# Smaller first units, row sums inverted on VectorE, normalisation in halves, and a new order of work in a planned attention and MLP kernel

## The chip, the core and the metric

The kernel runs on one core of a Trainium2 chip. Its engines have queues of their own: TensorE (PE in the profile; its weight loads are PEld), ScalarE (ACT), VectorE (DVE), GpSimd (POOL), and SyncE (SP), which only issues DMAs here. The metric is device time in microseconds, the median of several runs. A change of less than about 0.2%, or 1.5 us, can't be told from none.

## The reference

The input x has 2048 rows of 640 numbers. One branch is attention with 32 heads of 20 columns, the other an MLP with 1536 hidden columns and the activation mish. A sigmoid of x times a weight vector mixes them, row by row. All inputs are bf16.

```python
g = _sigmoid((x * gate_w).sum(-1, keepdims=True))
qkv = (x @ wqkv)...                                  # 32 heads of 20
scores = jnp.einsum("bhqd,bhkd->bhqk", q, k) * scale
p = _softmax(scores, axis=-1)
a = jnp.einsum("bhqk,bhkd->bhqd", p, v) ... @ wo
h = jnp.einsum("bsd,df->bsf", x, w1) + b1
b = jnp.einsum("bsf,fd->bsd", h * jnp.tanh(softplus(h)), w2)
return g * a + (1 - g) * b
```

The exponential of 32 x 2048 x 2048 scores is the bulk of the elementwise work.

## The kernel before

**Units and slots.** Heads are taken in 8 groups of 4 (`HG`), queries in 4 columns of 512 (`CW`). A group of a column, `(c, g)`, has 16 tiles of 128 keys. A *unit* `(c, g, kt, j)` is the score tile of head `j` for one tile of keys and the 512 queries: one matmul into one PSUM bank (`score_mms`, L1378). `subs` tells which matmuls a unit has. The last group is cut in two halves of 256 queries, and there a unit is 256 keys by 256 queries, made by two matmuls. Three units are a *slot*. There are 683 slots, and their scores take turns in banks 0 to 2 and 3 to 5.

**Who takes the exponential.** ACT takes a slot with one instruction (L1400), over three banks (1536 columns) or over two (1024). In the second case the slot's third unit was given to DVE by `choose`: DVE writes it as a 16-bit integer that is read as an fp16 number (`emit_x`, L1450). A batch of four such units gets two more passes over 2048 columns (`close`, L1488), since the value used is the sum of three such approximations. PE then multiplies by V (`pv`, L1720) into one bank for each group. A column of ones in V makes the row sums beside the products.

**Normalising a group** (`group_done`). DVE copies the bank to `OUNG` (L1905). A DMA collects the sums into `RR` (128x16). `invert` takes one over them: a power of -1 on GpSimd (L1927). A DMA writes `RR` to DRAM (`SUMS`), and four more spread it over the partitions into `BCT` (`spread`, L1936). One product `OUNG` x `BCT` follows, on DVE or on GpSimd (`times`, L1857). There is one `OUNG`. 31 groups go this way; the two cut halves at the end are transposed and inverted on DVE instead.

**The MLP's mish** is one tanh on ACT for each of 24 pieces (L1071), and then scalar steps (L1095) and four products (L1104) on 1024 fp16 columns. A product may be split in four: quarters to GpSimd, the rest to DVE.

**Who sets the order.** All of this is written out ahead of time. A planner (`Plan`) has a model of each engine's clock and adds instructions one by one. The numbers at the top of the file are its costs, due times and thresholds. `choose(s)` refuses to give a unit to DVE when DVE's modelled clock is too far ahead of ACT's: the variable `late` is DVE's lead less an allowance in `NUDGE`, one entry for each 8 slots. `settle` gives a job to GpSimd when it fits, by the modelled clocks, between two DVE instructions of kind "L" (those that work on SBUF alone) and would be done before DVE's modelled clock. `patient(op, wait)` holds DVE off from the same job until its clock is `wait` past the job's input: `AWAIT` (0) for the product with `BCT`, `AWAIT_2` (0.2) for a product of mish. `fill_up` puts matmuls into PE's idle time: while the streaming time that it modelled in the last `WINDOW` (4.8 us) is under `SPUN` (0.95) of it, and the filler bank is idle, it adds a matmul that nothing uses (`spin`, L2152).

**The start** (`first_keys`, `second_keys`). Two DMAs bring 256 rows of x each, PE turns them (L837), and DVE and ACT copy them to `XB` (L814 and L815). Then PE makes Q of group 0 for the low 256 rows and for the high 256, and K for the low 256 (L850). DVE copies K in two pieces of 128. The scores of slots 0 and 1 follow, then K of the high rows (`second_keys`, L818), then V of the first 512 rows (L887), and only then slot 2.

Of the kernel before, what the change touches and what calls it, by code (L numbers as in the profile page):

```python
# [17 lines left out]
P = 128  # L18
# [8 lines left out]
NFT = D // P  # L27
NFC = NF // P
NC = 4
CW = 512  # L30
NHC = 8
HW = 256
# [16 lines left out]
HOP = 0.1  # L49
# [5 lines left out]
STREAM = 0.38  # L55
SPUN = 0.95
# [6 lines left out]
PARTS = 1  # L63
MPARTS = 4
AWAIT_2 = 0.2
TAKE_M = 1
APART = 0.1
LANDED = 1.6
SEEN = 10
SPREAD_TAIL = 2.1  # L70
SUMS_TAIL = 1.1
FLEX = 1
TOP_UP = 0
SX = 305
SX_STEP = 1
AWAIT = 0
SHARE = 0.3
AWAIT_1 = 0
CALM_END = 90
# [12 lines left out]
GIVE_BACK = 50  # L92
# [6 lines left out]
STORED = 2  # L99
TALL = 0.1  # L100
BEYOND = 0.4
SOONER = 8
# [5 lines left out]
AHEAD = 20  # L108
# [6 lines left out]
CATCH_UP = 18  # L115
BUSY = 0.8
CROWD = 1.2
MARGIN = 2.5
EAGER = 85
LOAD = 0.95  # L120
MISH = 3.75
GROUP = 2.25
LAST = 0
END = 45
SHIFT = 0.6
LAG = 15
SPARE = 11
WINDOW = 4.8
# [11 lines left out]
OVER = 0  # L140
DIRECT = 1
FEW = 4
PART_DUE = 48
LAST_DUE = 29
# [21 lines left out]
NUDGE = [-5.3, -2.3, -2.8, 0.7, 4.4, 3.7, -3.0, 0.7, -3, 2.2, 2.2, -0.7, -0.7, 2.3, 0.8, -1.5, 4.5, 0.0, 6, 0, -0.7, -6, 0, 0, 2.1, 1.4, 0.7, 3.7, 0.7, 1.4, 5.2, 0.0, 4.4, 0, 4.7, 3, 3.7, 1.4, 6, 6, 6, 6, 2.3, 4.5, -0.8, -0.1, -0.8, 2.3, 0, 2.3, 1.4, 0, 2.2, 0, 0, 2.2, 1.5, 5, 2.9, 5.1, -0.8, 2.2, -3, 4.5, -5.7, -1.5, -0.1, -1, 4.5, 6, 6, 1.4, -4.3, 2.1, 4.9, 0.7, 0.7, 0.7, 0.0, -1.4, 5, 3.5, 6, 4.3, -1.5, -1.5, 1.5]  # L166
# [116 lines left out]
def bass_gated_mix__softmax_full_mha__dense_activation_mish__prompt_kernel(  # L283
# [154 lines left out]
    def attention(pl, fast):  # L438
# [97 lines left out]
        def safe(op):  # L536

            return op.t1 + HOP + RISK[op.eng]
# [78 lines left out]
        if fast:  # L617
# [206 lines left out]
            first_more = []  # L824

            def first_keys():
# [4 lines left out]
                def turn(half, pair):  # L831
# [9 lines left out]
                    by = ("dve", "act", "act") if half is lows else ("dve", "act", "dve")  # L841
# [6 lines left out]
                def mms(bank, pads, half, deps):  # L848
                    for f in range(NFT):
                        last = pl.add("pe", lambda e, f=f: e.matmul(  # L850
                            PS[:, bank, 0:HW], pads[:, 0, f, :], xt(0)[:, f, half], start=(f == 0), stop=(f == NFT - 1)),
                            [moved[(half is highs, f)], *deps], cost=HW * COL)
                    return last
# [17 lines left out]
                return pl.add("dve", lambda e: e.memset(PS[:, ACC, :], 1.0), [moved[(True, 4)]], cost=0.5)  # L871
# [157 lines left out]
            u_free = [None]  # L1029
# [36 lines left out]
            def mish(ev, hb, hc, k):  # L1066
# [9 lines left out]
                def piece(cost, fn, after=None, wait=0):  # L1076
                    def run(eng="dve", *more):
                        last[0] = pl.add(eng, fn, [last[0], *more], cost=ASIDE_1 if more else cost, kind="L")
# [9 lines left out]
                def done(op):  # L1088
                    h_done[(hc, k - 1)] = h_done[(hc, k)] = op
# [242 lines left out]
        def emit_s(s):  # L1332
            deps = [e_op.get(s - 2), ev_op.get(s - 2)]
            deps += [bank_free.get(SLOT * (s % 2) + i) for i in range(SLOT)] if s < 2 else []
            for c, g, kt, j in slots[s]:
                if fast:
                    deps += [k_done[(real(g), subs(c, g, kt)[-1][0] // 4)], q_done[(real(g), c)]]
                if fast and (c, g) == (0, 0) and 2 <= kt < 4:
                    deps += k_more
                if fast and s == 1:  # L1340
                    deps += first_more
# [24 lines left out]
        def score_mms(s, some, deps):  # L1366

            op = None
            for r in range(max(len(subs(*u[:3])) for u in some)):
                began = set()  # L1370
                for i, (c, g, kt, j) in enumerate(some):
# [3 lines left out]
                    cost = max(extent(c, g)[1] * COL, THIN)  # L1375
# [171 lines left out]
        def choose(s):  # L1547

            late = max(0.0, pl.now["dve"] - pl.now["act"]) - NUDGE[s // 8]
# [154 lines left out]
        def pv(some):  # L1704
# [3 lines left out]
            w = extent(c, g)[1]  # L1708
            bank = sums_at[(c, g)]
            for r in range(CW // w):  # L1710
                for n, ((_, _, kt, j), src, deps, scaled_v) in enumerate(some):
                    tile, cols, of_q = subs(c, g, kt)[r]
                    if not any(started.get((c, g, i)) for i in range(HG)):
                        deps = [*deps, bank_free.get(sums_at[(c, g)])]
                    if fast:
# [7 lines left out]
                        cost=0.004 if n else max(w * COL, THIN), kind="V")  # L1723
# [93 lines left out]
        def group_done(c, g, step, last):  # L1817
# [108 lines left out]
            def invert():  # L1926
                r = (pl.add("pool", lambda e: e.tensor_tensor(  # L1927
                    RR[:, :], RR[:, :], NEG[:, :].to_broadcast([P, 16]), ALU.pow), [got, m_neg], cost=INVERT)
                     if fast else pl.add("dve", lambda e: e.reciprocal(RR[:, :], RR[:, :]), [got], cost=0.25))
# [33 lines left out]
        if fast:  # L1963
# [3 lines left out]
            for s in range(2):  # L1967
                compose(s)
                emit_s(s)
# [455 lines left out]
```

## Time and profile before

| | |
|---|---|
| Median of 3 runs | 753.92 us (753.31 to 754.74) |
| Profiled execution: device time / span | 755.81 us / 754.0 us |
| ACT busy | 736.5 us, 98% |
| PE / DVE / POOL busy | 94% / 93% / 25% |
| Granted TensorE clock, mean | 0.998 |
| Exponentials on ACT: of 3 units / of 2 | 191 / 492 |
| Power of -1 on POOL | 31 times, 93.9 us |

In the groups of instructions, the name of a row is the line, the engine, the operation, and what is written from what. After the count stand the busy time, the mean nanoseconds of one, and the engine's idle time just before. Instructions of one engine overlap at their ends, so the step from start to start is shorter than the duration. In the chain of waits, a row is a piece of the work that ended last, with start and length. In a table by stretches, the numbers beside an engine are its busy time and its count.

### The profile page before, as it was taken

Reading aid. Unit: us, or ns where it says so; the run is one execution under the profiler, and the core shown is the slowest. Engines: PE = TensorE matmul, PEld = TensorE weight load, DVE = VectorE, ACT = ScalarE, POOL = GpSimd, SP = SyncE. Lnnn points to the kernel's source line nnn. Section 1 sums busy time; section 2 is a strip of 40 time slices with the busy share of each in tenths; the row PEclk is TensorE's granted clock in tenths of the full one; section 3 lists DMA queues with packets and bytes.
Section 4 is the critical chain, followed back from the end, with each engine's and each line's share of the span. In section 5 each row is a group of like instructions: output and inputs, shape, how many; then the busy total and the mean of one; then the engine's idle time right before and its main releaser. Section 6 shows DMA issues by size and latency. Waiting matters only on the chain.

```text
span 754.0 us, 19649 instructions
## 1 busy us (share of the span) xinstructions
PE 707.4 (94%) x8065; PEld 266.4 (35%) x8065; DVE 703.4 (93%) x1298; ACT 736.5 (98%) x715; POOL 188.6 (25%) x162
## 2 busy tenths in 40 slices
PE   8999999999998999999999999999999999999996
PEld 4334333333332343233333334333333333323232
DVE  4878898999898999989999999999999999999995
ACT  6999999999999999999999999999999999999996
POOL 8111101333212420212213322213204232223111
PEclk9999999999999999999999999999999999999999
DMA  8321321321233215112113302102222122011001
GB/s 188 105 63 42 99 70 35 101 67 53 65 107 101 70 47 163 39 42 56 54 44 108 95 21 73 60 21 76 82 55 71 55 60 80 20 33 31 18 18 47
DMA packets 81675, 49.62 MB, mean 66 GB/s; under 512 B 25474, under 2 KB 77562, under 8 KB 81578
## 3 DMA queue, kind: packets, MB, share of 16 engines
q1 hardware_dynamic: 80810, 48.16, 22.7%
q8 instruction: 67, 1.10, 0.6%
q14 instruction: 30, 0.25, 0.1%
q10 hardware_dynamic: 656, 0.10, 0.1%
q0 software_dynamic: 112, 0.01, 0.0%
HBM read 36.10 MB, written 7.52 MB: 58 GB/s over the span
## 4 chain that ended last, share of the span: by engine, by line
ACT 86%; PE 7%; DVE 3%; DMA 2%; POOL 0%; issue 0%; SPq 0%
ACT ETS L1400 83%; ACT REG L1071 2%; PE PS L1378 2%; PE PS L1720 2%; PE PS L575 2%; ACT W2R L1071 1%; DVE QT L1450 1%; DMA OTN<-in_A_x_dram 1%; DMA SUMS<-RR 1%; DMA BCT<-SUMS 1%; DVE KT L1450 0%; PE PS L785 0%; POOL RR L1927 0%; DMA RR<-OUNG 0%; PE PS L2152 0%
## 5 line engine op out<-in xcount | busy, mean ns | idle before, releaser
L1400 ACT ACTIVATE ETS<-PS 128x1024 bf16<-128x1024 f32 (+1 forms) x683 | 715.7, 1263 | 5.4 <-PE PS L1378 4.9
L1378 PE MATMUL PS<-QT,KT 32*128 32x512 bf16 (+1 forms) x2112 | 267.3, 378 | 34.0 <-ACT ETS L1400 23.7
L1927 POOL TENSOR_TENSOR RR<-RR,NEG 128x16 f32<-128x16 f32 x31 | 93.9, 3029 | 268.8 <-DMA RR<-OUNG 268.8
L1720 PE MATMUL PS<-ETS,V_all 128*21 128x512 bf16 (+1 forms) x1606 | 156.8, 375 | 0.0
L1378 PEld LDWEIGHTS PS<-QT,KT 32*128 32x128 bf16 x2112 | 67.7, 91 | 250.4 <-ACT ETS L1400 212.1
L1104 POOL TENSOR_TENSOR U<-U 128x256 f16<-128x256 f16 x77 | 50.9, 661 | 215.6 <-DVE U L1095 176.8
L1450 DVE TENSOR_SCALAR QT<-PS 128x512 int16<-128x512 f32 x123 | 82.4, 682 | 2.6 <-PE PS L1378 1.9
L575 PE MATMUL PS<-XB,REG 128*32 128x256 bf16 (+3 forms) x824 | 80.5, 294 | 2.0 <-DVE OUTT L1185 1.5
L1450 DVE TENSOR_SCALAR OTN<-PS 128x512 int16<-128x512 f32 x109 | 73.3, 681 | 2.3 <-PE PS L1378 2.0
L575 PE MATMUL PS<-W2R,HB 128*128 128x320 bf16 (+1 forms) x645 | 72.4, 300 | 0.2
L1450 DVE TENSOR_SCALAR PADS<-PS 128x512 int16<-128x512 f32 x101 | 67.9, 682 | 4.8 <-PE PS L1378 4.6
L575 PEld LDWEIGHTS PS<-XB,REG 128*32 128x32 bf16 (+1 forms) x824 | 39.5, 97 | 32.1 <-issue 21.1
L1720 PEld LDWEIGHTS PS<-ETS,V_all 128*21 128x21 bf16 x1606 | 39.1, 90 | 30.0 <-issue 25.5
L575 PEld LDWEIGHTS PS<-W2R,HB 128*128 128x128 bf16 (+1 forms) x645 | 33.1, 97 | 29.1 <-issue 14.7
L1450 DVE TENSOR_SCALAR KT<-PS 128x512 int16<-128x512 f32 x54 | 36.7, 684 | 4.0 <-PE PS L1378 3.7
L1104 DVE TENSOR_TENSOR U<-U 128x1024 f16<-128x1024 f16 (+3 forms) x71 | 38.6, 544 | 0.0
L1450 DVE TENSOR_SCALAR REG<-PS 128x512 int16<-128x512 f32 x56 | 38.0, 682 | 0.1
L1048 DVE TENSOR_TENSOR HB<-PS,B1T 128x512 bf16<-128x512 f32 x48 | 32.7, 681 | 0.4 <-PE PS L575 0.2
L1095 DVE TENSOR_SCALAR U<-U 128x1024 f16<-128x1024 f16 x72 | 30.1, 418 | 0.5
L1488 DVE TENSOR_SCALAR QT<-QT 128x2048 int16<-128x2048 int16 (+2 forms) x43 | 28.6, 667 | 0.7 <-PE PS L1720 0.7
L1104 POOL TENSOR_TENSOR HB<-U,HB 128x256 bf16<-128x256 f16 x28 | 18.7, 669 | 38.1 <-DVE U L1104 25.6
L1720 PE MATMUL PS<-QT,V_all 128*21 128x512 f16 x280 | 28.2, 388 | 0.0
(176 smaller groups left out, 801.8 us busy)
## 6 DMA issues: line engine op xcount, KB each, us to landing
REG<-in_B_w_dram SPq DMA_DIRECT2D x36, 320.0 KB, 3.2
BCT<-SUMS SPq DMA_DIRECT2D x124, 64.0 KB, 2.0
W2R<-in_B_w_dram SPq DMA_DIRECT2D x12, 320.0 KB, 3.4
KT<-KS SPq DMA_DIRECT2D x28, 128.0 KB
QT<-QS SPq DMA_DIRECT2D x112, 20.0 KB
QS<-WOQ SPq DMA_DIRECT2D x16, 128.0 KB, 1.7
KS<-OTN SPq DMA_DIRECT2D x16, 128.0 KB, 2.6
W2R<-in_B_w_dram SPq DMA_DIRECT2D x1, 1920.0 KB, 8.3
```

The source lines that it names most:

```text
L575: op = e.matmul(PS[at, bank, cols], w[:, at], x, start=start, stop=stop, **({"tile_position": (0, i * rows)} if parts > 1 else {}))
L1048: ev = dve(lambda e: e.tensor_tensor(hb, PS[:, bank, :].rearrange("p (i t) -> p i t", i=2), bias, ALU.add), [last, b_load, *b_read.get(hc ...
L1071: ex = pl.add("act", lambda e: e.activation(U, h, AF.Tanh, scale=0.5, bias=-MISH_AT), [ev, u_free[0]], cost=0.95)
L1095: return lambda e: e.tensor_scalar(dst, src, *ops)
L1104: return lambda e: e.tensor_tensor(dst[:, at], one[:, at], two[:, at], ALU.mult)
L1378: op = pl.add("pe", lambda e, i=i, g=real(g), tile=tile, j=j, cols=cols, c=c, of_q=of_q: e.matmul(scores(s)[:, i, cols], KT[32 * j:32 * j ...
L1400: e_op[s] = pl.add("act", lambda e: e.activation(EXPS[:, at:at + n, :], scores(s)[:, 0:n, :], AF.Exp, scale=SCALE, bias=LIFT if fast else ...
L1450: ev = dve_by(lambda e: e.tensor_scalar(block(batch["y"], n, I16), scores(s)[:, 2, :], SCALE * ULPS, BIAS, ALU.mult, ALU.add), [s_op[s], * ...
L1488: op = pl.add("dve", lambda e, sp=sp: e.tensor_scalar(some_of(home, sp, I16), some_of(y, sp, I16), by, None, ALU.add), deps, cost=each, ki ...
L1720: lasts[n] = pl.add("pe", lambda e, v=v, j=j, src=src[:, cols], of_q=of_q, count=count: e.matmul(PS[32 * j:32 * j + EW, bank, of_q], v, sr ...
L1927: r = (pl.add("pool", lambda e: e.tensor_tensor(RR[:, :], RR[:, :], NEG[:, :].to_broadcast([P, 16]), ALU.pow), [got, m_neg], cost=INVERT) ...
```

## The change

- **First units.** Of column 0, group 0, the first two units of each head become 256 keys by 256 queries: unit `kt` = 0 is the low half of the queries, unit 1 the high half, each over the first two tiles of keys. `pv` and `score_mms` take each unit's own width.
- **The start.** PE now makes Q low, K low, four of the five steps of Q high (into the bank `ACC`), the scores of slot 0, the fifth step of Q high, and then the scores of slot 1, which wait for the copy of Q high. Q low is copied by ACT, K low by DVE in one piece of 256 columns, Q high by DVE. One copy of x moves from ACT to DVE. K high and V stand behind slot 1, as before.
- **Sums.** `ON_DVE`: `invert` is a DVE reciprocal of `RR` in place of POOL's power.
- **Halves.** `PARTS` = 2: the product with `BCT` can go to POOL in halves of 256 columns. `AWAIT` is 3 and `AWAIT_2` is 0.8.
- `DIRECT` = 2: column 3, group 6 is also transposed and inverted on DVE, without the DMAs, which leaves 30 groups with DMAs.
- In mish each step also waits for the end of the product chain of the piece before (`formed`).
- **Order.** `NUDGE` has an entry for each 4 slots, with new values. `SPUN` is 0.5, `STREAM` 0.42, `WINDOW` 6. Some thirty more thresholds and due times of the planner are new, so all five engines' orders are.

```diff
-STREAM = 0.38
-SPUN = 0.95
+STREAM = 0.42
+SPUN = 0.5
...
-PARTS = 1
+PARTS = 2
...
-AWAIT_2 = 0.2
+AWAIT_2 = 0.8
...
+EARLY_Q = 4
+RISK_SP = 0.6
+ON_DVE = 1
...
-SPREAD_TAIL = 2.1
-SUMS_TAIL = 1.1
+SPREAD_TAIL = 1.8
+SUMS_TAIL = 0.8
...
-AWAIT = 0
+AWAIT = 3
...
-WINDOW = 4.8
+WINDOW = 6
...
-DIRECT = 1
+DIRECT = 2
...
             n = CW // w
+            if fast and (c, g) == (0, 0) and kt < 2:
+                return [(t, (lows, highs)[t], (lows, highs)[kt]) for t in range(2)]
             return [(kt * n + i, slice(i * w, (i + 1) * w), slice(at, at + w)) for i in range(n)]
...
-                    by = ("dve", "act", "act") if half is lows else ("dve", "act", "dve")
+                    by = ("dve", "act", "dve")
...
                 low = mms(5, PADQ, lows, [pad(0, 0)])
-                last = mms(0, PADQ, highs, [])
-                pad_read[(0, 0)] = last
+                last = mms(FB, PADK, lows, [pad(1, 0)])
+                q, k = QT[:, 0, 0:CW], KT[:, 0, 0:CW]
+                q_low.append(copy("act", q[:, lows], PS[:, 5, 0:HW], low, 0.36))
+                bank_free[5] = q_low[0]
+                k_done[(0, 0)] = bank_free[FB] = copy("dve", k[:, lows], PS[:, FB, 0:HW], last, 0.36)
+                mms(ACC, PADQ, highs, [moved[(True, 4)]], range(0, EARLY_Q))
+                compose(0)
+                emit_s(0)
+                pad_read[(0, 0)] = last = mms(ACC, PADQ, highs, [], range(EARLY_Q, NFT))
                 wq_read.append(last)
-                q, k = QT[:, 0, 0:CW], KT[:, 0, 0:CW]
-                bank_free[5] = copy("dve", q[:, lows], PS[:, 5, 0:HW], low, 0.36)
-                q_done[(0, 0)] = bank_free[0] = copy("act", q[:, highs], PS[:, 0, 0:HW], last, 0.36)
-                pad_read[(1, 0)] = last = mms(FB, PADK, lows, [pad(1, 0)])
-                first = copy("dve", k[:, 0:P], PS[:, FB, 0:P], last, 0.2)
-                bank_free[FB] = copy("dve", k[:, P:HW], PS[:, FB, P:HW], last, 0.2)
-                k_done[(0, 0)] = first
-                first_more.append(bank_free[FB])
+                q_done[(0, 0)] = copy("dve", q[:, highs], PS[:, ACC, 0:HW], last, 0.36)
...
-            late = max(0.0, pl.now["dve"] - pl.now["act"]) - NUDGE[s // 8]
+            late = max(0.0, pl.now["dve"] - pl.now["act"]) - NUDGE[s // 4]
...
                 r = (pl.add("pool", lambda e: e.tensor_tensor(
                     RR[:, :], RR[:, :], NEG[:, :].to_broadcast([P, 16]), ALU.pow), [got, m_neg], cost=INVERT)
-                     if fast else pl.add("dve", lambda e: e.reciprocal(RR[:, :], RR[:, :]), [got], cost=0.25))
+                     if fast and not ON_DVE else pl.add("dve", lambda e: e.reciprocal(RR[:, :], RR[:, :]), [got], cost=0.17))
...
-            for s in range(2):
-                compose(s)
-                emit_s(s)
+            compose(1)
+            emit_s(1)
             second_keys()
             task = v_task(0, 0, -1)
```

More of the change, by code (lines that the diff above doesn't have):

```diff
@@ L107 @@
 ALL = 0.42
-AHEAD = 20
+AHEAD = 5
 SPREAD = 1
@@ L1077, in run @@
                     def run(eng="dve", *more):
-                        last[0] = pl.add(eng, fn, [last[0], *more], cost=ASIDE_1 if more else cost, kind="L")
+                        last[0] = pl.add(eng, fn, [last[0], *more, *formed], cost=ASIDE_1 if more else cost, kind="L")
                         if after:
@@ L1374, in score_mms @@
                     tile, cols, of_q = subs(c, g, kt)[r]
-                    cost = max(extent(c, g)[1] * COL, THIN)
+                    cost = max((of_q.stop - of_q.start) * COL, THIN)
                     if j in began:
@@ L1707, in pv @@
             lasts = {}
-            w = extent(c, g)[1]
             bank = sums_at[(c, g)]
-            for r in range(CW // w):
+            for r in range(max(len(subs(*u[:3])) for u, *_ in some)):
+                ran = 0
                 for n, ((_, _, kt, j), src, deps, scaled_v) in enumerate(some):
+                    if r >= len(subs(c, g, kt)):
+                        continue
                     tile, cols, of_q = subs(c, g, kt)[r]
+                    w = of_q.stop - of_q.start
                     if not any(started.get((c, g, i)) for i in range(HG)):
```

65 lines of the change are left out of this document (33 added, 32 removed).

## The prediction, as it was put on record

> **What bounds the kernel now.** I read the page first.
>
> ```profile
> span 754.0 us, 19649 instructions
> PE 707.4 (94%) x8065; PEld 266.4 (35%) x8065; DVE 703.4 (93%) x1298; ACT 736.5 (98%) x715; POOL 188.6 (25%) x162
> ```
>
> ```profile
> ACT 86%; PE 7%; DVE 3%; DMA 2%; POOL 0%; issue 0%; SPq 0%
> ```
>
> ACT is busy for 98% of the span and makes up 86% of the chain that ended last. So the time is the start up to the first exponential, then ACT's instructions one behind the other, then a tail. To see what ACT's line is made of I took the groups of instructions with shapes apart, in the whole run and in two stretches where nearly one shape stands alone (300.4 to 311.2 us, then 37.6 to 44.1 us).
>
> ```profile
> L1400 ACT ACTIVATE ETS<-PS 128x1024 bf16<-128x1024 f32 x492 | 494.4, 1141 | 1.6 <-PE PS L1378 1.4
> ```
>
> ```profile
> L1400 ACT ACTIVATE ETS<-PS 128x1024 bf16<-128x1024 f32 x12 | 11.2, 1145 | 0.0
> ```
>
> ```profile
> L1400 ACT ACTIVATE ETS<-PS 128x1536 bf16<-128x1536 f32 x5 | 7.0, 1624 | 0.0
> ```
>
> Twelve exponentials of two units take 11.2 us, so one step is (11.2 - 1.1)/11 = 0.92 us. One of three units steps in (7.0 - 1.6)/4 = 1.35 us. Each unit that DVE takes off ACT saves 0.43 us, and 492 of 683 slots have given one. What keeps the other 191? The table by stretches tells:
>
> ```profile
> 60.00:100.00 40.00, 38.20 (x464) 14.72 (x462) 33.87 (x66) 40.00 (x39) 5.79 (x2) 1.00 0.27 81
> ```
>
> ```profile
> 540.00:580.00 40.00, 37.67 (x454) 15.47 (x449) 39.90 (x80) 40.00 (x39) 11.89 (x11) 1.00 0.22 60
> ```
>
> The columns are PE, PEld, DVE, ACT and POOL busy. In the second row ACT and DVE are both full (40.00 and 39.90 of 40), and POOL has 28 us left. Early on DVE has 6 us to spare. So ACT and DVE bound the kernel together: time taken off DVE is worth something only if the new order turns it into more units taken off ACT.
>
> What is that worth? A unit costs DVE one L1450, and a quarter of two L1488 passes:
>
> ```profile
> 341.00 0.68 DVE L1488 TENSOR_SCALAR QT<-QT 128x2048 int16<-128x2048 int16 x1
> 341.60 0.68 DVE L1450 TENSOR_SCALAR OTN<-PS 128x512 int16<-128x512 f32 x1
> ```
>
> Steps on a full DVE are 0.60 us, so a unit costs 0.60 + 2 x 0.60/4 = 0.90 us. If r us are freed, both engines end sooner by t when (t + r')/0.90 units move, with r' the part of r so spent and t = r - r' = 0.43 x r'/0.90. So t = r x 0.43/(0.43 + 0.90) = **0.32 r**.
>
> **The start.** The timelines of PE, DVE and ACT:
>
> ```profile
> 6.53 1.41 PE L850 MATMUL PS<-XB,WOQ 128*128 128x256 bf16 x10
> 7.77 0.71 PE L850 MATMUL PS<-XB,REG 128*128 128x256 bf16 x5
> 8.95 0.61 PE L1378 MATMUL PS<-QT,KT 32*128 32x512 bf16 x6 [0.48 <-DVE KT L815]
> 9.49 0.72 PE L818 MATMUL PS<-XB,REG 128*128 128x256 bf16 x5
> 10.82 0.88 PE L887 MATMUL PS<-REG,XB 128*128 128x80 bf16 x20 [0.61 <-DVE KT L815]
> 11.63 0.39 PE L1378 MATMUL PS<-QT,KT 32*128 32x512 bf16 x3
> 12.23 0.39 PE L1378 MATMUL PS<-QT,KT 32*128 32x512 bf16 x3 [0.21 <-ACT ETS L1400]
> 12.56 0.61 PE L575 MATMUL PS<-XB,REG 128*128 128x512 bf16 x2
> ```
>
> ```profile
> 8.51 0.49 DVE L815 CAST KT<-PS 128x128 bf16<-128x128 f32 x2 [0.67 <-PE PS L850]
> ```
>
> ```profile
> 10.25 0.42 DVE L815 CAST KT<-PS 128x256 bf16<-128x256 f32 x1 [0.66 <-PE PS L818]
> ```
>
> ```profile
> 9.39 11.14 ACT L1400 ACTIVATE ETS<-PS 128x1536 bf16<-128x1536 f32 x9 [1.05 <-PE PS L1378]
> ```
>
> The text says that the first slot needs half the rows of x. But both halves' turning still stands ahead of every projection in PE's order, so the second half's DMA is waited for as before, and 6.53 stays. K low now takes the place of Q high and ends at 6.53 + 1.41 = 7.94, not at 8.48. Its copy of 256 columns takes 0.42, so to 8.39 with 0.03 to notice. From a copy's end to PE's next start it is 10.82 - 10.67 = 0.15, so scores at 8.54. From first score to exponential it is 9.39 - 8.95 = 0.44: the first exponential starts at 8.98, **0.41 sooner**.
>
> What is late next is slot 2. Behind slot 0 on PE now stands Q high's last step (at +0.33, as 12.23 to 12.56, so 8.87 to 9.14), then slot 1, which waits for its copy (to 9.60, PE at 9.75). K high follows at 10.08 and takes 0.72, its copy ends at 11.25, V starts at 11.40, and slot 2's scores come 0.81 behind V's start (11.63 - 10.82), at 12.21. ACT gets them at 12.65. Before, it took its third exponential at 9.39 + 2 x 1.35 = 12.09. So I take the start as a **loss of 0.6**. The ends are -0.4 (the lead is kept, if PE catches up from later slack) and +0.6.
>
> **DVE's account.**
>
> ```profile
> 738.13 0.20 DVE L1889 RECIPROCAL U<-U 128x8 f32<-128x8 f32 x1
> 738.37 0.45 DVE L1890 STREAM_TRANSPOSE U<-U 128x256 f32<-128x256 f32 x1
> ```
>
> ```profile
> L1857 DVE TENSOR_TENSOR OTN<-OUNG,BCT 128x512 bf16<-128x512 f32 x27 | 18.4, 681 | 1.9 <-DMA BCT<-SUMS 1.9
> L1104 DVE TENSOR_TENSOR U<-U 128x1024 f16<-128x1024 f16 x26 | 17.7, 680 | 0.0
> ```
>
> ```profile
> L1104 DVE TENSOR_TENSOR U<-U 128x512 f16<-128x512 f16 x22 | 9.1, 414 | 0.0
> ```
>
> ```profile
> L1104 POOL TENSOR_TENSOR U<-U 128x256 f16<-128x256 f16 x77 | 50.9, 661 | 215.6 <-DVE U L1095 176.8 <-DVE OTN L1857 10.9 <-DVE OTN L1488 9.4
> L1104 POOL TENSOR_TENSOR HB<-U,HB 128x256 bf16<-128x256 f16 x28 | 18.7, 669 | 38.1 <-DVE U L1104 25.6 <-DVE QT L1488 5.0 <-DVE OTN L1488 3.6
> L1857 POOL TENSOR_TENSOR OTN<-OUNG,BCT 128x512 bf16<-128x512 f32 x3 | 3.8, 1269 | 16.1 <-DMA BCT<-SUMS 16.1
> ```
>
> - *Reciprocals.* 30 come to DVE. 128x8 takes 0.20 and the next starts 0.24 after. So +6.0 to +7.2; I take 6.0. The POOL powers that go were off the chain, and their time is free for the rest.
> - *Products with BCT.* 27 are on DVE, at steps of 0.60: 16.2. A whole one takes POOL 1.27, longer than two of DVE's steps, and so rarely fits between two "L" instructions. A half is about the 0.66 of POOL's other 256 columns and fits beside two steps; and DVE now holds off for 3 us. I take three quarters moved, -12.2; ends 0 (POOL's share stays) and -16.2.
> - *Mish products.* POOL has 77 + 28 = 105 quarters of 24 x 4 x 4 = 384. A quarter saves DVE (680 - 414)/2 = 133 ns. DVE held off for 0.2 and holds for 0.8 now; a quarter takes POOL 0.66. I take 60 more, -8.0; ends 0 and -14 (as many again).
> - *Column 3, group 6* on DVE: the transposes are 0.45 for 256 columns, so about 0.8 for 512 (estimate), twice, and its product: +2.3.
>
> Net r = 12.2 + 8.0 - 6.0 - 2.3 = 11.9, so 0.32 x 11.9 = **3.8 us sooner**. The ends are r = -9.5 (3.0 later) and r = 21.9 (7.0 sooner). The new waits on `formed` are covered by the gap between mish pieces: 24 pieces in some 550 us.
>
> **The waits for sums.** DVE's order is fixed, so a product or reciprocal that waits for a DMA holds all behind it: first the L1450 that free PSUM banks, then PE's scores, then ACT. Before, this happened once (chain, DVE's and ACT's timelines):
>
> ```profile
> 229.64 4.12 DMA SUMS<-RR
> ```
>
> ```profile
> 235.07 3.85 DMA BCT<-SUMS
> ```
>
> ```profile
> 238.94 0.69 DVE L1857 TENSOR_TENSOR OTN<-OUNG,BCT 128x512 bf16<-128x512 f32 x1 [1.89 <-DMA BCT<-SUMS]
> ```
>
> ```profile
> 240.81 1.45 ACT L1400 ACTIVATE ETS<-PS 128x1536 bf16<-128x1536 f32 x1 [1.54 <-PE PS L1378]
> ```
>
> With 3 us of patience this one goes: -1.5. But 30 reciprocals now wait on DVE for `RR`, which POOL waited for at no cost. At the old rate of one slip in 27, that is 30/27 x 1.54 = +1.7; the ends are 0 and the rival below. Net +0.2.
>
> **The sum.** 0.6 - 3.8 + 0.2 = -3.0. The tail (last exponential to the end) does the same work. That the order is new in itself I price at 0, from -2.3 to +2.3: the page's row for L1400 has ACT idle for PE for 4.9 us, and 4.9 - 1.05 - 1.54 = 2.3 stand beside the first exponential's wait and the one quoted.
>
> ```profile
> L1400 ACT ACTIVATE ETS<-PS 128x1024 bf16<-128x1024 f32 (+1 forms) x683 | 715.7, 1263 | 5.4 <-PE PS L1378 4.9
> ```
>
>  Against the profiled execution, 755.81 with 754.0 of span, this gives 752.8 and 751.0. Its span nearly equals the unprofiled median of 753.92, so the forecast for the median is **750.9 us**.
>
> **The rivals.**
>
> *POOL takes all it is offered* (r = 21.9): 0.6 - 7.0 + 0.2, so 747.7, and 746 if the start also keeps its lead and no reciprocal slips. For it: POOL has 28 of 40 us left even with its powers. Against it: a half still needs two steps of DVE without an "L" instruction.
>
> *The relief isn't used.* PE bounds some stretches (38.20 of 40 at 60 to 100 us, where DVE had 6 us idle and yet no more units went). If as many units as before go to DVE, 0.6 + 0.2 remain: 754.7, no change to be measured.
>
> *Reciprocals behind late DMAs: slower.* Place: the first 345 us, where SP and the DMA engines carry the weights. Timelines of SP and POOL:
>
> ```profile
> 295.19 0.79 SPq L1923 DMA_DIRECT2D RR<-OUNG  x1
> ```
>
> ```profile
> 303.09 2.89 POOL L1927 TENSOR_TENSOR RR<-RR,NEG 128x16 f32<-128x16 f32 x1 [26.94 <-DMA RR<-OUNG]
> ```
>
> Here the sums took 7.9 us to arrive. POOL didn't mind; DVE would if the planner's clock has it there earlier. Each slip costs ACT 1.54 by the row above. Two more slips take the forecast's gain. From three on it is slower by more than can be told from no change: 750.9 + 3 x 1.54 = 755.5, and 758.6 with five. Against it: the planner models SP's queue, and 27 waits of the same kind slipped once.
>
> *The clock.* By stretches, with PE's busy time first and the granted clock as the 1.00 and 0.50, then ACT's timeline, then the fillers (L2152) by stretches:
>
> ```profile
> 310.60:314.02 3.42, 1.96 (x24) 0.50 (x20) 3.28 (x8) 3.42 (x4) 0.00 (x0) 1.00 0.02 1
> 314.02:317.44 3.42, 3.42 (x30) 0.81 (x28) 2.66 (x5) 2.37 (x3) 0.00 (x0) 0.50 0.10 16
> ```
>
> ```profile
> 317.05 4.20 ACT L1400 ACTIVATE ETS<-PS 128x1024 bf16<-128x1024 f32 x4 [1.05 <-PE PS L1378]
> ```
>
> ```profile
> 600.00:700.00 100.00, 5.53 (x20) 1.38 (x20) 1.00 0.17 48
> ```
>
> After 3.42 us with PE busy for 1.96, the clock was halved for 3.42 us, and ACT lost 1.05. Now `SPUN` is 0.5 and most of the late fillers, 20 in these 100 us, may go. Five such drops would cost 5.3: 756.2. *TensorE: Matmul & The Clock Gate* of the Trainium skill (Why this matters for your kernels) asks only for no PE gaps over some 3 us; by it fewer fillers cost nothing. The trace disagrees: this drop had no such gap.
>
> **Chances.** Forecast (748.5 to 752.4): 0.42. POOL takes all: 0.20. Relief not used: 0.19. Late DMAs: 0.11. Clock: 0.08. The first two are faster by more than 1.5 us, about what can be told from no change, with a part of the third: 0.65 faster, 0.18 the same, 0.17 slower. Range: 746.3 (the second case's low end) to 756.0, which leaves out most of the slow cases.
>
> **What would show it.** Right: the first exponential near 9.0 and the third near 12.6; L1857 on POOL with 256 columns, some 45 of 60; over 492 exponentials of 1024 columns, by some 9 (3.8/0.43); the idle before 240.81 gone. Wrong: L1857 mostly on DVE; idle DVE before a reciprocal with the DMA `RR` as its releaser; clock under 1.00 late in the run; a count near 492.

## The result, and the profile after

The change made the kernel slower. Measured side by side on one chip, the kernel before took 754.74 us (753.31 to 758.24) and the changed one 759.16 us (756.15 to 764.08): a ratio of **1.0053**, 95% interval 1.0030 to 1.0076. The profiled execution took 761.89 us, 2.7 above that median, so what it shows is somewhat larger than the typical loss. The head of its page and its chain of waits:

```profile
span 760.1 us, 19480 instructions
PE 712.0 (94%) x7982; PEld 265.4 (35%) x7982; DVE 700.2 (92%) x1310; ACT 739.7 (97%) x713; POOL 111.8 (15%) x160
...
ACT 84%; PE 11%; DVE 3%; DMA 1%; issue 0%; SPq 0%; DVEq 0%
```

ACT still bounds the kernel, but PE has 11% of the chain where it had 7%. The groups of instructions, shapes apart (busy time, mean ns, then the idle time before):

```profile
L1405 ACT ACTIVATE ETS<-PS 128x1024 bf16<-128x1024 f32 x485 | 492.7, 1133 | 3.8 <-PE PS L1383 3.5
L1405 ACT ACTIVATE ETS<-PS 128x1536 bf16<-128x1536 f32 x198 | 308.0, 1580 | 4.9 <-PE PS L1383 2.9 <-PE PS L1728 1.9
L1110 POOL TENSOR_TENSOR U<-U 128x256 f16<-128x256 f16 x92 | 59.9, 651 | 299.1 <-DVE U L1101 199.6 <-DVE OTN L1866 26.7 <-DVE QT L1493 21.6
L1110 POOL TENSOR_TENSOR HB<-U,HB 128x256 bf16<-128x256 f16 x28 | 18.7, 668 | 68.9 <-DVE U L1110 46.6 <-DVE QT L1493 8.9 <-DVE OTN L1866 6.8
L1866 POOL TENSOR_TENSOR OTN<-OUNG,BCT 128x256 bf16<-128x256 f32 x19 | 13.8, 725 | 213.7 <-DVE PADS L1493 69.7 <-DMA BCT<-SUMS 66.5 <-DVE OUTT L2062 46.6
L1866 DVE TENSOR_TENSOR OTN<-OUNG,BCT 128x512 bf16<-128x512 f32 x18 | 12.3, 686 | 2.4 <-DMA BCT<-SUMS 2.4
L1938 DVE RECIPROCAL RR<-RR 128x16 f32<-128x16 f32 x30 | 7.4, 246 | 1.2 <-DMA RR<-OUNG 1.2
L1866 DVE TENSOR_TENSOR OTN<-OUNG,BCT 128x256 bf16<-128x256 f32 x5 | 2.1, 419 | 0.0
```

Seven slots fewer gave a unit to DVE (485 for 492). POOL took 19 halves of the products and 120 quarters of mish, and DVE still makes 18 products whole. ACT's timeline at the start and at the end, of the kernel after and then of the end of the one before:

```profile
8.95 2.79 ACT L1405 ACTIVATE ETS<-PS 128x1536 bf16<-128x1536 f32 x2 [1.10 <-PE PS L1383]
12.55 2.79 ACT L1405 ACTIVATE ETS<-PS 128x1536 bf16<-128x1536 f32 x2 [0.81 <-PE PS L1383]
...
736.85 16.40 ACT L1405 ACTIVATE ETS<-PS 128x1536 bf16<-128x1536 f32 x13
```

```profile
734.42 11.99 ACT L1400 ACTIVATE ETS<-PS 128x1536 bf16<-128x1536 f32 x9
```

These split the 6.1 us between the two spans. The first exponential starts 9.39 - 8.95 = 0.44 sooner. The last one ends at 753.25, after 746.41; behind it remain 6.85 us where there were 7.59, another 0.74 gained. Seven units more on ACT cost 7 x 0.43 = 3.0. That leaves 6.1 + 0.44 + 0.74 - 3.0 = 4.3 us. Most of it, 3.3, is idle time on ACT, and 0.6 is longer tanh instructions (28.9 us for 28.3). The waits of ACT and DVE for one releaser (total, times, longest):

```profile
ACT ETS L1405 <- PE PS L1383: 6.3, 11, 1.1
ACT ETS L1405 <- PE PS L1728: 1.9, 1, 1.9
```

```profile
DVE OTN L1866 <- DMA BCT<-SUMS: 2.4, 1, 2.4
DVE RR L1938 <- DMA RR<-OUNG: 1.2, 1, 1.2
```

ACT waits 8.2 us for scores and V products where it waited 4.9, which are the 3.3. The longest of it starts with the 2.4 us on DVE. From the timeline of all engines there:

```profile
307.67 2.20 SPq L756 DMA_DIRECT2D QT<-QS  x6
309.92 0.35 SPq L1939 DMA_DIRECT2D SUMS<-RR  x1
311.39 1.69 SPq L1945 DMA_DIRECT2D BCT<-SUMS  x4
314.89 0.69 DVE L1866 TENSOR_TENSOR OTN<-OUNG,BCT 128x512 bf16<-128x512 f32 x1 [2.40 <-DMA BCT<-SUMS]
317.12 0.61 PE L1383 MATMUL PS<-QT,KT 32*128 32x512 bf16 x3 [2.07 <-DVE REG L1455]
318.30 1.45 ACT L1405 ACTIVATE ETS<-PS 128x1536 bf16<-128x1536 f32 x1 [1.86 <-PE PS L1728]
320.56 1.94 ACT L1405 ACTIVATE ETS<-PS 128x1024 bf16<-128x1024 f32 x2 [0.81 <-PE PS L1383]
```

SP issues the sums' transfers behind loads of Q. DVE stands 2.40 us in front of a product; the L1455 behind it frees PE's bank late, PE stands for 2.07, and ACT for 1.86 and 0.81. The table by stretches shows why there are two gaps (the first number behind the stretch is its length, then PE's busy time; after POOL's, the granted clock):

```profile
286.43:289.85 3.42, 2.95 (x28) 1.02 (x24) 3.42 (x9) 3.42 (x5) 0.00 (x0) 1.00 0.21 60
313.74:317.15 3.41, 0.99 (x15) 0.56 (x14) 2.16 (x4) 2.70 (x3) 0.00 (x0) 1.00 0.10 23
317.15:320.56 3.41, 3.41 (x30) 0.89 (x30) 1.95 (x5) 1.45 (x1) 0.00 (x0) 0.50 0.12 26
327.39:330.80 3.41, 2.02 (x17) 0.58 (x13) 3.34 (x8) 2.82 (x4) 0.84 (x2) 1.00 0.12 33
330.80:334.22 3.42, 3.42 (x29) 0.58 (x30) 2.23 (x5) 2.43 (x4) 0.00 (x0) 0.50 0.11 27
```

PE was busy for 0.99 of 3.41 us, and got half its clock for the next 3.41. So this wait on DVE was paid twice: once as the wait, once as a slow stretch behind it. It isn't always so. In the kernel before, DVE waited 1.89 us at 238.94, PE was busy for 1.96 of the 3.41 us from 238.93, and the clock stayed at 1.00.

### The profile page after: what moved, and what is told of

It reads as the page before. It is cut to its first block, busy times and chain, and to the rows that moved or that the text cites. A ratio compares the mean times of both kernels' runs of the same rounds, so it can differ in the third digit from the quotient of the medians.

```text
span 760.1 us, 19480 instructions
## 1 busy us (share of the span) xinstructions
PE 712.0 (94%) x7982; PEld 265.4 (35%) x7982; DVE 700.2 (92%) x1310; ACT 739.7 (97%) x713; POOL 111.8 (15%) x160
## 4 chain that ended last, share of the span: by engine, by line
ACT 84%; PE 11%; DVE 3%; DMA 1%; issue 0%; SPq 0%; DVEq 0%
ACT ETS L1405 81%; PE PS L1383 3%; PE PS L1728 3%; ACT REG L1076 2%; PE PS L580 2%; PE PS L2160 1%; ACT W2R L1076 1%; DMA OTN<-in_A_x_dram 1%; DVE QT L1455 0%; PE PS L962 0%; PE PS L919 0%; DMA BCT<-SUMS 0%; DMA RR<-OUNG 0%; DVE REG L1455 0%; DVE QT L1493 0%
## 5 line engine op out<-in xcount | busy, mean ns | idle before, releaser
L1110 POOL TENSOR_TENSOR U<-U 128x256 f16<-128x256 f16 x92 | 59.9, 651 | 299.1 <-DVE U L1101 199.6
L1455 DVE TENSOR_SCALAR QT<-PS 128x512 int16<-128x512 f32 x128 | 86.4, 684 | 4.3 <-PE PS L1383 3.9
L1455 DVE TENSOR_SCALAR OTN<-PS 128x512 int16<-128x512 f32 x105 | 71.0, 686 | 4.0 <-PE PS L1383 3.2
L580 PE MATMUL PS<-W2R,HB 128*32 128x320 bf16 (+1 forms) x627 | 71.5, 300 | 0.8 <-DVE WOQ L801 0.6
L1455 DVE TENSOR_SCALAR PADS<-PS 128x512 int16<-128x512 f32 x88 | 59.6, 686 | 4.9 <-PE PS L1383 4.8
L1866 POOL TENSOR_TENSOR OTN<-OUNG,BCT 128x256 bf16<-128x256 f32 x19 | 13.8, 725 | 213.7 <-DVE PADS L1493 69.7
L1455 DVE TENSOR_SCALAR REG<-PS 128x512 int16<-128x512 f32 x62 | 42.0, 685 | 3.0 <-PE PS L1383 3.0
L580 PEld LDWEIGHTS PS<-W2R,HB 128*32 128x32 bf16 (+1 forms) x627 | 33.0, 97 | 29.4 <-issue 15.4
L1455 DVE TENSOR_SCALAR KT<-PS 128x512 int16<-128x512 f32 x51 | 34.8, 685 | 2.7 <-PE PS L1383 2.6
L1110 DVE TENSOR_TENSOR U<-U 128x768 f16<-128x768 f16 (+3 forms) x70 | 36.6, 523 | 0.0
L580 PE MATMUL PS<-XB,WOQ 128*32 128x512 bf16 (+1 forms) x164 | 28.3, 406 | 0.0
```

What stands on the lines that cost most here:

```text
L580: op = e.matmul(PS[at, bank, cols], w[:, at], x, start=start, stop=stop, **({"tile_position": (0, i * rows)} if parts > 1 else {}))
L1110: return lambda e: e.tensor_tensor(dst[:, at], one[:, at], two[:, at], ALU.mult)
L1455: ev = dve_by(lambda e: e.tensor_scalar(block(batch["y"], n, I16), scores(s)[:, 2, :], SCALE * ULPS, BIAS, ALU.mult, ALU.add), [s_op[s], * ...
L1866: op = pl.add(eng, lambda e: e.tensor_tensor(to[:, cols], src[:, cols], BC[:, cols], ALU.mult), [*deps, *reads()], cost=WIDE * share + 0.0 ...
```

## The experiments

Ratios are against the kernel before on the same chip. All but the re-planned ones keep the order in which the planner wrote the instructions; they change the finished list.

### Single suspects

**e1: the reciprocal alone, in the kernel before.**

```diff
+                if fast:
+                    r.eng = r.key = "dve"
+                    r.fn = lambda e: e.reciprocal(RR[:, :], RR[:, :])
```

> The kernel before with its whole order of work kept, except that the 31 inversions of the row sums are DVE reciprocals where they were POOL powers. Theory A (the reciprocals cost DVE time where DVE is full): 31 x 0.25 = 7.8 us more on DVE, of which the half that falls where DVE has no idle time shows: 2 to 4 us slower than before, DVE busy near 711. Theory B (DVE waits for the DMA of the sums, and PE and ACT behind it): over 4 us slower, with idle DVE before the reciprocals, its releaser the DMA into RR, of more than 3 us in all. Theory C (the reciprocals are not the cause): within 1.5 us of before, since the sums now come 2.7 us sooner.

Ratio **1.0046** (1.0024 to 1.0067), nearly the whole loss. That is some 3.5 us, which the range of theory A holds; but the trace shows the waits of theory B, 2.6 us for `RR` (it asked for over 3) and 2.3 for `BCT`, where the kernel before had 1.9 for `BCT`. DVE's timeline, then ACT's:

```profile
112.53 0.25 DVE L1932 RECIPROCAL RR<-RR 128x16 f32<-128x16 f32 x1 [2.01 <-DMA RR<-OUNG]
```

```profile
114.47 3.28 ACT L1400 ACTIVATE ETS<-PS 128x1024 bf16<-128x1024 f32 x3 [1.36 <-PE PS L1378]
119.09 1.02 ACT L1400 ACTIVATE ETS<-PS 128x1024 bf16<-128x1024 f32 x1 [1.34 <-PE PS L1378]
```

Again two gaps for one wait: the clock was halved from 115.65 to 119.06. The two, 2.7 us, are about the difference of the spans, 756.8 to 754.0.

**e2: the kernel before without its 51 fillers.**

```diff
+    fast.ops = [op for op in fast.ops if op not in spins]
```

> The kernel before with its whole order kept, but without the 51 filler matmuls. Theory A (they hold the TensorE clock): more half-clock stretches late in the run, each some 2.4 us by the slope of time against granted clock over the changed kernel's runs; two more give 759. Theory B (they are not needed): time and granted clock as before, 754 to 755.

Ratio 1.0000 (0.9983 to 1.0018). The mean granted clock of its runs is a little lower, 0.9955 for 0.9979, and the time is the same: the fillers hold up no clock that matters.

**e3 and e4: the scores of slots 270 to 299 (after: to 304) made twice**, to fill PE's gaps there.

```diff
+            if fast and PAD[0] <= s < PAD[1]:
+                pads[pl.ops[n_ops]] = pl.ops[n_ops:]
```

> The kernel before with its order kept, and every score matmul of slots 270 to 299 (some 300 to 332 us) made twice, so that PE streams 0.2 us more in each slot. Theory A (the half-clock stretch at 314 us costs time of its own): no such stretch, granted clock 1.000, 1 to 2.5 us faster than before. Theory B (the stretch is a mark of PE waiting, and costs nothing itself): the clock at 1.000, but the time as before or up to 2 us slower for the extra matmuls.

> The changed kernel with its order kept, and every score matmul of slots 270 to 304 (some 300 to 339 us) made twice. Theory A (the clock is what spreads the times and half of the loss): no half-clock stretch at 317 and 331 us, runs close together near 756 us, some 3 us under the changed kernel's median of 759.2. Theory B (the wait of DVE for the late sums at 315 us is the loss, and the clock only follows): the stretch stays, or the time stays near 759.

Ratios 1.0050 (1.0031 to 1.0069) and 1.0093 (1.0072 to 1.0115), slower by about 0.4 to 0.5% each. The clock stayed at 0.998 to 1.000 in every run, and the runs of e3 lie within 1.4 us of each other, those of e4 within 0.7; but the padding costs more than the half-clock stretches did. Both missed what was expected, and since the extra matmuls cost time themselves, neither tells what a half-clock stretch costs.

**e5: slot 2's scores ahead of V, after.**

```diff
+    first = [op for op in fast.ops if op is marks["e0"] or op in marks["s2"]]
...
+    fast.ops[v0:v0] = first
```

> The changed kernel with its order kept, but the first exp and the scores of slot 2 stand ahead of the V product of group 0 on TensorE. Theory A, the later third exp is carried to the end: the third exp starts near 11.7 instead of 12.55, and the time falls by 0.8 us against the changed kernel, to a ratio of 1.004 against the kernel before. Theory B, the 0.8 us are used up behind the start because ScalarE there waits for TensorE anyway: the third exp starts near 11.7, the idle time comes back on ScalarE before 40 us, and the ratio stays within 0.001 of 1.0053. If V's chunk is now late for the first O product, ScalarE is idle for longer than before in the first 40 us and the ratio rises to 1.0065.

Ratio 1.0061 (1.0039 to 1.0083): no gain, though the gap ahead of the third exponential is gone (four in a row from 9.34). As theory B has it, the idle time comes back: ACT waits 0.27, 0.22, 0.41 and 0.54 us in what follows, and its tenth exponential starts at 22.11, in the changed kernel's execution at 21.38. In its profiled execution the sums at 314.89 came in time, there was no half-clock stretch before the tail, and the span was 756.4 for the same 485 units. So the wait at 314.89 and what hangs on it are some 3.7 us between these two executions; the median of e5 is no better.

### What a wait costs

**e6: as e1, each reciprocal and its transfer three DVE instructions later.**

```diff
+    for r in recs:
+        i = fast.ops.index(r)
...
+        fast.ops[i:j] = fast.ops[i + 2:j] + moved
```

> The kernel before with its order, the inversions of the sums on VectorE as in e1_recip_only, but each of them (and SyncE's transfer of the result behind it) three VectorE instructions later. Theory A, the loss of e1 is the wait of VectorE behind a late transfer of sums (2.01 us at 112.53 and the half-clock stretch behind it): the waits on RR vanish, no half-clock stretch near 115, and the ratio falls from 1.0046 to between 0.999 and 1.002. Theory B, the loss is VectorE's own time (31 inversions of 0.246 us, 7.6 us, at 0.32 to 0.45 us each per us): the ratio stays at 1.0035 to 1.0046 although no wait on RR is seen. If the sums come too late for the products of BCT, VectorE waits for BCT instead, with the same price in another place: 1.003 or more, and waits <-BCT of over 1 us in the trace.

Ratio 1.0076 (1.0053 to 1.0099). The waits for `RR` went (0.2 us is left), and the products behind now waited, as the third case has it:

```profile
DVE OTN L1858 <- DMA BCT<-SUMS: 6.8, 4, 3.3
```

**e7: after, the inversions back on POOL as powers.**

```diff
+                if fast:
+                    r.eng = r.key = "pool"
+                    r.fn = lambda e: e.tensor_tensor(RR[:, :], RR[:, :], NEG[:, :].to_broadcast([P, 16]), ALU.pow)
```

> The changed kernel with its order, but the inversions of the sums back on GpSimd as a power (2.9 us each instead of 0.25), so VectorE has neither the 7.4 us of them nor the wait of 1.18 us on RR. Theory A, the inversions carry the loss also here as they did in the kernel before (0.46% there): the ratio falls to 1.000 to 1.002. Theory B, the loss of the changed kernel is elsewhere (its order: 485 instead of 492 units of exp on VectorE, and the wait for the sums at 314.89): the ratio stays at 1.004 to 1.006, because the sums now land 2.7 us later and VectorE waits for BCT instead (at 314.89 for 5 us instead of 2.40).

Ratio 1.0134 (1.0108 to 1.0161), outside both expectations. DVE now waits for POOL's pieces, which stand behind the powers, and for `BCT`:

```profile
DVE U L1110 <- POOL U L1110: 5.9, 6, 1.7
DVE OTN L1866 <- DMA BCT<-SUMS: 3.6, 2, 2.1
DVE OTN L1866 <- POOL OTN L1866: 1.6, 2, 1.3
DVE HB L1110 <- POOL HB L1110: 1.3, 1, 1.3
```

So it doesn't tell what the inversions cost in the changed kernel. That needed a run in which nothing else becomes late:

**e9: after, without any inversion.**

```diff
+    for r, got in dropped:
+        fast.ops.remove(r)
```

> The changed kernel with its order, and its 30 inversions of the sums left out altogether, on every engine (the sums are spread as they are, so the output is not divided by them). VectorE has 7.4 us less work and no wait on RR. Theory A, VectorE's load and its wait for the sums are the loss: the ratio falls from 1.0053 to 1.001 or less, as the loss of e1_recip_only (0.46%) is given back. Theory B, the loss lies in the order, in which VectorE has 485 units instead of 492 and ScalarE 3.0 us more of exp, whatever VectorE is spared afterwards: the ratio stays at 1.004 or more.

Ratio 1.0025 (1.0003 to 1.0046), between the two theories: by the ratios, the 30 reciprocals with all the waits that hang on them are about half of the loss, though the intervals of this run and the changed kernel overlap. The other half fits DVE's 485 units. In the profiled execution DVE waits for no sums, and the span is 755.9, 1.9 above that of the kernel before. The seven units give +3.0; the first exponential at 8.80 gives -0.59, the tail of 6.72 us gives -0.87, and ACT's waits behind the first exponential, 4.0 for 3.9, give +0.1: together +1.6 of the 1.9.

**e10 and e11: the products with `BCT` all on POOL**, after and before. Those that need no DMA stay on DVE.

```diff
+    for op in products:
+        op.eng = op.key = "pool"
```

> The changed kernel with its order, but all products of BCT that VectorE makes (23 but for the last ones, some 14 us; one of them waits 2.40 us for BCT at 314.89) are made by GpSimd in their places. Theory A, VectorE's load and waits in the order as it is are the loss: the wait at 314.89 and the half-clock stretches behind it are gone, the ratio falls from 1.0053 to 0.999 to 1.002. Theory B, the loss lies in the division fixed by the order (ScalarE's 3.0 us more of exp): the ratio is 1.003 to 1.005. If GpSimd then holds up quarters of the mish that VectorE waits for: waits of VectorE <-POOL of 3 us or more and a ratio over 1.006.

> The kernel before with its order, and VectorE's products of BCT (27 of 31, 18 us, with the wait of 1.89 us at 238.94) made by GpSimd in their places. Theory A, time of VectorE that is freed without a new order gives 0.32 us per us, as in the prediction: 18 us less give 5.8 us, ratio 0.993. Theory B, freed time gives only what waits it takes away, since the division of exp between ScalarE and VectorE is fixed in the order: 1 to 2 us, ratio 0.997 to 0.999. Theory C, GpSimd, which also has 31 inversions of 3.0 us each, comes late with products and quarters: waits of VectorE or TensorE on GpSimd, ratio over 1.002.

e10: 1.0079 (1.0048 to 1.0110), not better than the changed kernel. That is in the range of the third case, but DVE waits for POOL for only 0.6 us there; what else made it slow is open. e11: 0.9986 (0.9972 to 1.0001), about 1 us that can't be told from none (2.1 at the interval's end), for 18 us of DVE's work and its wait. DVE waits there neither for sums nor for POOL. Time freed on DVE is worth next to nothing while the order stays: the number of units is fixed in it.

### The order

**e8 and e12: other lists of `NUDGE`**, found by a search in the planner's own count of the time (which is no measurement), after and before.

```diff
-NUDGE = [-0.3, -6, -2.3, ...
+NUDGE = [...
```

> The changed kernel with everything of the change kept but for its order: another list of due-time shifts (NUDGE) for the same blocks of background work. Theory A, the order is what the change lost by: by the count of the program 488 of 690 units of 1024 columns go to VectorE or the whole ends some 6 us earlier, so the time falls to 752 to 755, ratio 0.996 to 1.000. Theory B, what the change adds (inversions on VectorE, products of BCT kept there for three fifths) is what it lost by, in any order: 757 to 760, ratio 1.003 to 1.007. A ratio between is a part of each.

> The kernel before, nothing of the change, but another list of due-time shifts: by the count of the program it ends 3.4 us earlier, with 496 units on VectorE instead of 491. Theory A, a new order is worth what the program counts: ratio 0.994 to 0.998. Theory B, a new order costs a few us against one that has been chosen by its time, whatever the program counts (as e8_after_order, 6 us earlier by the count and 3 us later on the chip): ratio 1.001 to 1.008, with new waits of VectorE on sums (<-RR or <-BCT) or half-clock stretches that the kernel before hasn't.

e8: 1.0083 (1.0059 to 1.0108), with 489 units and 5.4 us of waits for `RR`. Some 2 us of it lie outside the span: its device time is 3.3 to 4.1 us over the span in every run, for 1.8 in the kernel before, and why is open. e12: 1.0000 (0.9984 to 1.0017). Both are outside what either theory gave. In e12 the last exponential ended 3.6 us earlier than before, at 742.84, and all of it was lost in the tail. There four of the last pieces of the projection went over ACT and POOL in turn, one waiting for the other, where the kernel before has one such piece:

```profile
744.70 0.94 ACT L1250 ACTIVATE PADS<-PS,GATE 128x320 f32<-128x320 f32 x2 [1.86 <-PE PS L575]
746.27 0.53 ACT L1250 ACTIVATE PADS<-PS,GATE 128x320 f32<-128x320 f32 x1 [0.62 <-POOL HB L1253]
747.90 0.53 ACT L1250 ACTIVATE PADS<-PS,GATE 128x320 f32<-128x320 f32 x1 [1.10 <-POOL HB L1253]
```

So the search was done again with the whole end as its aim, for both structures (e13, e15), and for the changed one with patience for the reciprocal (e14: the planner may place it only 1.5 us after it expects the sums):

```diff
-            norm.append((0.25, invert, lambda: got))
+            norm.append((0.25, invert, lambda: False if fast and patient(got, 1.5) else got))
```

> Everything of the change, with another list of due-time shifts, found by the count of the whole end (tail with it), 491 units on VectorE by that count. Theory A, the order of the change is what loses the rest: 752 to 756, ratio 0.995 to 1.000, and not slower than e15_before_order2 by more than 0.002. Theory B, the pieces cost their 2 to 4 us in any order: ratio 1.003 or more, slower than e15_before_order2 by 0.003 or more.

> As e13_after_order2, with an order made for it in the same way, but an inversion may only be placed on VectorE 1.5 us after its sums are expected to land. Theory A, VectorE's waits for sums are what the inversions cost: no wait <-RR of over 0.5 us, granted clock of the runs higher than in e13, ratio lower than that of e13 by 0.002 or more. Theory B, it is VectorE's time: the same ratio as e13 within 0.0015. If the sums now come to the products too late, waits <-BCT of 1 us or more take the place of those <-RR, and the ratio is that of e13 or worse.

> The kernel before, nothing of the change, with an order found as that of e13_after_order2 (494 units on VectorE by the count). Theory A, orders found by the same search differ on the chip by what the structures differ in: 752 to 755, ratio 0.996 to 1.000. If a new order alone costs some us against the one that the kernel came with, the ratio is 1.002 or more, and the part of the change's loss that e9_after_no_recip leaves (0.25%) is that of any new order.

e13: **0.9999** (0.9984 to 1.0014). Everything of the change, in another order and with 492 units, loses nothing. It does so with 4.4 us of waits for `RR`, more than the changed kernel's 3.6 for `RR` and `BCT`, and with the clock at 1.00 up to the tail. e15: 0.9986 (0.9971 to 1.0001). e14: **0.9966** (0.9953 to 0.9980), 752.78 us, faster than both kernels; its eleven runs lie within 1.1 us, at a mean clock of 0.9995 for e13's 0.9981. That is theory A's gain, though a wait of 0.8 us for `RR` is left. What differs between e13 and e14, as DVE's waits (e13's row first) and ACT's groups (e14):

```profile
DVE RR L1938 <- DMA RR<-OUNG: 4.4, 2, 2.9
```

```profile
DVE RR L1938 <- DMA RR<-OUNG: 1.5, 2, 0.8
```

```profile
L1405 ACT ACTIVATE ETS<-PS 128x1024 bf16<-128x1024 f32 x494 | 493.6, 1136 | 1.4 <-PE PS L1383 0.9
```

**e16: the order of e14, the reciprocals three DVE instructions earlier.** e14's list is another one than e13's, so this run keeps e14's list and moves each reciprocal forward, with the transfer of its result.

```diff
+    for r, got in recs:
+        i = fast.ops.index(r)
...
+        fast.ops[j:i + 2] = moved + fast.ops[j:i]
```

> The order of e14_after_patient, but each of the 30 inversions, with the transfer of its result behind it, stands three VectorE instructions earlier (never ahead of the load that it waits for). Theory A, patience is the gain: VectorE waits for RR in more than five places, over 5 us in all, and the ratio rises from 0.9966 to 1.000 or more. Theory B, the list of shifts is the gain: waits for RR may come back, but the ratio stays below 0.998.

Ratio **1.0126** (1.0100 to 1.0152): 11.9 us of span, from the place of 30 instructions of 0.25 us and the transfers behind them. DVE's waits and ACT's:

```profile
DVE RR L1939 <- DMA RR<-OUNG: 12.0, 9, 2.6
```

```profile
ACT ETS L1406 <- PE PS L1384: 13.2, 17, 2.1
```

The runs that share an order give the price of DVE's waits for sums (`RR` and `BCT`):

| Pair | DVE's waits, us | Span, us | Span per us waited |
|---|---|---|---|
| before to e1 | 1.9 to 4.9 | 754.0 to 756.8 | 0.9 |
| before to e6 | 1.9 to 7.0 | 754.0 to 760.7 | 1.3 |
| after to e9 | 3.6 to 0 | 760.1 to 755.9 | 1.2 |
| e14 to e16 | 1.5 to 12.0 | 750.6 to 762.5 | 1.1 |
| after to e5 | 3.6 to 1.3 | 760.1 to 756.4 | 1.6 |
| after to e10 | 3.6 to 1.5 | 760.1 to 759.0 | 0.5 |
| before to e11 | 1.9 to 0 | 754.0 to 754.4 | -0.2 |

Each row compares two single executions, and those of one kernel differ by several us (754.4 to 762.3 of span for the changed one). Where the waits differ by 3 us or more, the price is 0.9 to 1.3; where they differ by some 2 us, it can't be read. The first three rows hold the reciprocals' own 7.4 us as well, the fourth doesn't, and their prices agree. So with the order kept it is the waits that cost, about 1.1 us for each us, and the work costs nothing that shows.

## Why the prediction was wrong

Forecast 750.9 us, measured 759.2, which is beyond the range's end of 756.0. By its own steps:

- **What bounds the kernel: right in part.** ACT's line is the kernel, and units moved are the currency. But the rule of 0.32 us per us of DVE freed could hold only if the order turns the time into units; e11 freed 18 us and got about 1, where the rule gives 5.8. The planner's list decides, not the engine's time.
- **The start: right in kind, in part by luck, and of no use.** Forecast 8.98 for the first exponential and 12.65 for the third, measured 8.95 and 12.55. But the first exponential lies between 8.75 and 9.34 in the ten profiled executions with the new start, 9.02 in the mean, and between 8.89 and 9.50 in the eight with the old one, 9.21 in the mean. The lead is rather 0.2 than 0.41. The loss was still there at the tenth exponential (21.38, before 20.91), and closing the gap gained nothing (e5).
- **The relief, r = 11.9 for -3.8: the step that failed first.** Forecast were some 45 halves of 60 on POOL, it was 19; 60 more quarters, it was 15 more; +6.0 for the reciprocals, it was 7.4. The products took DVE 18.4 us before and 12.3 + 2.1 after: 4.0 freed, not 12.2. A quarter saves 0.133, so 15 of them 2.0, not 8.0. Column 3, group 6 measured 2.3, as forecast. So r = 4.0 + 2.0 - 7.4 - 2.3 = **-3.7**, by the rule of 0.32 1.2 us later and not 3.8 sooner. DVE was not relieved but loaded. Its busy time bears this out: it fell by only 3.2 us (703.4 to 700.2) while seven units, 6.3 us at 0.90, left it. I had taken "three quarters moved" from the length of a half beside two of DVE's steps; that such a place comes up within 3 us of the sums' landing was assumed from nothing.
- **The order at 0, from -2.3 to +2.3: the step that failed second.** Three orders for the same pieces measured 1.0083 (2 us of it outside the span), 1.0053 and 0.9999, some 4 to 6 us apart. The one that came with the change gave ACT 3.0 us more of exponentials. I had bounded it by ACT's idle time, which can't hold it: an order that moves fewer units leaves ACT busy, not idle.
- **The waits for sums, +0.2: kind right, size wrong.** The new wait for `RR` came (1.18 us at 112.26). The old one for `BCT` didn't go in spite of 3 us of patience; it moved to 314.89 and grew to 2.40. A slip was priced at 1.54 for 1.89 us, 0.8 per us; the table gives about 1.1, half-clock stretches included. The waits grew by 1.7 us, so about 1.9 at that price, where 0.2 was taken; by e5 the one place at 314.89 made more of it in the profiled execution.
- **The rivals.** "Reciprocals behind late DMAs" (0.11) named the mechanism that e1 and e16 show, and its place, the first 345 us. It gave 755.5 to 758.6 with three to five slips; there were two, one of them of a product, and the order's loss on top. "The clock" (0.08) was right that a stretch with PE half idle can be followed by half the clock; the 1.96 us of PE that it quotes were, the same 1.96 from 238.93 were not. The rule set beside it, no PE gaps over some 3 us (*TensorE: Matmul & The Clock Gate* of the Trainium skill, Why this matters for your kernels), isn't enough here: PE stood for 2.07 us at the longest before 317.15, and the clock was halved; the measurement decides. Another section of that page of the Trainium skill (A second HAM failure mode: psum-queue depth-cycling) does describe a kernel in which frequent short idle times between groups of matmuls made the clock go up and down, and with that the rows agree. The rival was wrong about the place: not the late run, where the changed kernel has 30 fillers between 600 and 700 us for 20, and where fillers don't matter anyway (e2), but the stretches behind DVE's waits. "POOL takes all" and "relief not used" both failed on the same number: there was no relief.
- **What would show it.** Of the signs named for "wrong" three came: products mostly on DVE (18 whole and 5 halves), idle DVE before a reciprocal, and a count of 1024-column exponentials not above 492 (485).

Not settled: how much of the 0.33% of e14 is the change and how much the better list, since e15 has half of that with nothing of the change and the intervals of the two overlap. How the loss divides between the waits and the order is known only about (e9), and the halves, the new waits on `formed` and the new start were not taken back one by one; e13 only shows that together they need not cost anything.

## What to carry to other kernels

Where an engine's instructions run in a fixed order, as DVE's do here, a short instruction that waits for a DMA costs what it waits, not what it takes: here about 1.1 us of the end per us waited, for instructions of 0.25 us. Before moving such a step from an idle engine to a full one, give it a place well behind its data, and give what uses its result a later place too: moved alone, the reciprocals passed the wait on to the products (e6). With a new list, 30 reciprocals placed later turned a loss of 0.5% into a gain of 0.3%. And where a planner writes the order, a change's gain can't be read from engine times alone: compare the structures under orders that were found in the same way.

## What the runs showed of the hardware

The granted clock fell to 0.50 for 3.41 us (6.83 us once, in e6) in each case ahead of the tail, after a stretch of 3.41 us in which PE was busy for 0.50 to 2.22 us; after 2.95 busy, in the changed kernel's row from 286.43, it stayed at 1.00. No pause of the whole engine as long as that was needed: 2.02 us of short matmuls with gaps between them were followed by it too. But PE's busy time doesn't settle it. Stretches that fall on the same steps of 3.41 us and have PE busy for 1.96 us (before, from 238.93), 1.86 (e7, from 726.05) and 2.01 (e6, from 318.84) were followed by a clock of 1.00. What tells the two kinds apart is open.

Time and clock go together between runs: over the 13 runs of the changed kernel the span was 754.4 to 755.7 us at a mean clock of 0.999 and 762 at 0.992. Whether the clock makes the difference, or the waits that leave PE idle, these runs don't tell.
